# The last pair of token tiles in a seven-product block multiplication: its own order of products and PSUM tiles, and its stores halved between two queues

## The chip, the cores and the metric

The kernel runs on one core of a Trainium2 chip. The metric is the device time of one execution in microseconds (us); times of several runs are given as their median with the lowest and the highest. One further execution was recorded by the hardware profiler. All times inside it are counted from the start of its span, which runs from the first instruction to the last.

## The reference

An attention stage feeds a two-layer feed-forward stage. Batch 8, 12 heads, 448 tokens, head width 64; 3584 tokens of width 768 in all, inner width 2048.

```python
q_n, k_n = (rmsnorm(q, g_q), rmsnorm(k, g_k))
scores = scale * np.matmul(q_n, k_n.transpose(0, 1, 3, 2))
attn = softmax(scores)                      # max taken off, sums divided
x = np.matmul(attn, v)                      # then heads side by side: (B*S, H*D)
h = x @ w_in
g = np.maximum(h, 0.0) + alpha * np.minimum(h, 0.0)
out = (g @ w_out).astype(np.float32)
```

(`softmax` is written out in the reference.) The change touches only the last product, `g @ w_out`, for the last tokens.

## The kernel before

The order of all work is written out by hand: the kernel is traced under a manual schedule, and a planner ahead of the main loop spreads the feed-forward matmuls over the attention steps by estimated costs. Each engine runs its instructions in the program's order, and so does each queue of DMA issues. Loads and most stores are issued by SyncE (SP).

Feed-forward, first half (`up`, L475 to L498): for one block of 128 inner columns, TensorE (PE) makes `hT`, ScalarE (ACT) scales it by alpha, VectorE (DVE) takes the maximum, and the result is a row block of `gT`, held as 16 blocks of 128 inner columns by 896 tokens (two batches). Second half (`down`, L500): a tile of 128 tokens times a half of the output columns (384), 16 matmuls summed in one PSUM bank, copied to `osb` and stored.

For the last two batches, output tiles t = 1 to 6 are done another way, in pairs (1, 2), (3, 4) and (5, 6). Before them the remaining `up` blocks run, with what is left of tile 0, done the ordinary way, mixed in (L815 to L820, L1029). A pair of token tiles and the two halves of the inner columns make a 2 x 2 block matrix, the two halves of the inner columns and the two halves of the output columns another, and `quad` (L576) multiplies them by a Strassen-Winograd scheme: seven block products in place of eight. GpSimd (POOL) makes the sums of the weight blocks once (`mix_weights`, L537) and the sums s1 to s4 of the token blocks for each pair (`mix`, L559).

A block product (`product`, L600) is 8 matmuls of 128 x 128 by 128 x 384, issued at L602, into one PSUM bank. Two of the seven add onto a bank that holds an earlier product. Numbered as in the new code, with the order that `quad` has before (L614 to L641):

- m1: block (t, 0) times the first weight block, into bank x. ACT copies it to SBUF (L616).
- m6: s2 into bank y. DVE adds the copy and gives u2 (L619).
- m5: s1 into bank p, or, in the last pair, in two halves of 192 columns into two banks (`ps`).
- m7: s3 into bank z. DVE adds u2 and gives u3 (L624).
- m2: onto x. ACT copies it into an output tile (L627): output of tile t, left half. Two stores.
- then p + u3, with no product of its own (L631): output of tile t + 1, right half. Two stores.
- m4: onto z. DVE adds u2 (L635): output of tile t + 1, left half. Two stores.
- m3: s4 onto p. DVE adds u2 (L640): output of tile t, right half. Two stores; in the last pair it goes by halves of 192 columns, each with its own addition and two stores.

`send` (L568) stores a tile as two DMAs of 64 partitions each (L572): 96 KB each, 48 KB for a half of the columns. All are issued by SP, except that with `split` the second is issued by ACT; before the change only m3's halves in the last pair have that.

```python
(nc.scalar if split and half else nc.sync).dma_start(
    out=dst[:, c], in_=o[ds(64 * half, 64), c]
)
```

PSUM tiles come from three pools: `pss` (tag `sc`, two buffers of two banks), `psa` (tag `acc`, one buffer of two banks), `psf` (tag `mm`, two buffers of one bank). Pairs 1 and 5 take x, p from one `sc` tile and y, z from the other; pair 3 takes y, z from `acc` and x, p from `mm`. A reused buffer makes its first writer wait for the last reader of the tile before. The output tiles `osb` have four buffers; a buffer is free when its stores have landed.

The pairs run in the order 1, 3, 5 (L1033 to L1034), and nothing comes after pair 5.

Of the kernel before, what the change touches and what calls it, by code (L numbers as in the profile page):

```python
# [9 lines left out]
FP32 = mybir.dt.float32  # L10
# [11 lines left out]
def kernel(  # L22
# [12 lines left out]
    nc = tc.nc  # L35
# [9 lines left out]
    OH = DM // 2  # L45
# [14 lines left out]
    psa = ctx.enter_context(tc.tile_pool(name="psa", bufs=1, space=bass.MemoryType.PSUM))  # L60
# [495 lines left out]
    def block(t, f):  # L556
        return gT[:, ts(f, HF), ts(t, 128)]
# [10 lines left out]
    def send(b0, t, oh, o, c=slice(0, None), split=False):  # L568
        for half in range(2):
            bb, j = divmod(2 * t + half, J)  # L570
            dst = out4[b0 + bb, j, :, ts(oh, OH)]
            (nc.scalar if split and half else nc.sync).dma_start(  # L572
                out=dst[:, c], in_=o[ds(64 * half, 64), c]
            )

    def quad(b0, t, wide, last=False):  # L576

        s1, s2, s3, s4 = (mixes[t][:, n] for n in range(4))
        if wide:
            even, odd = (  # L580
                pss.tile([128, 2, 512], FP32, name="oq", tag="sc") for _ in range(2)
            )
            x, p = even[:, 0], even[:, 1]
        else:
            odd = psa.tile([128, 2, 512], FP32, name="oqa", tag="acc")
            x, p = (psf.tile([128, 512], FP32, name="oqm", tag="mm") for _ in range(2))
        y, z = odd[:, 0], odd[:, 1]
        full = (slice(0, OH),)
        ps = [p]
        if last:  # L590
            full = (slice(0, OH // 2), slice(OH // 2, OH))
            ps = [psf.tile([128, 512], FP32, name="oqm", tag="mm") for _ in range(2)]

        def whole(f, m):
            return lambda ft: w_out_sb[:, HF * f + ft, ts(m, OH)]

        def mixed(n):
            return lambda ft: tw[n, ft // QF][:, ft % QF]

        def product(bank, g, v, first, c=slice(0, OH)):  # L600
            for ft in range(HF):
                nc.tensor.matmul(  # L602
                    out=bank[:, c], lhsT=g[:, ft], rhs=v(ft)[:, c],
                    start=(first and ft == 0), stop=(ft == HF - 1),
                    skip_group_check=True,
                )

        def part(name):
            return ld.tile([128, OH], FP32, name=name, tag="qs", bufs=4)

        def result():
            return ffn.tile([128, OH], FP32, name="osb", tag="osb", bufs=4)

        product(x, block(t, 0), whole(0, 0), True)  # L614
        m1 = part("m1")
        nc.scalar.copy(out=m1, in_=x[:, :OH])  # L616
        product(y, s2, mixed(1), True)
        u2 = part("u2")
        nc.vector.tensor_add(out=u2, in0=y[:, :OH], in1=m1)  # L619
        for b, c in zip(ps, full):  # L620
            product(b, s1, mixed(0), True, c)
        product(z, s3, mixed(2), True)
        u3 = part("u3")
        nc.vector.tensor_add(out=u3, in0=z[:, :OH], in1=u2)  # L624
        product(x, block(t, 1), whole(1, 0), False)
        o = result()
        nc.scalar.copy(out=o, in_=x[:, :OH])  # L627
        send(b0, t, 0, o)
        o = result()
        for b, c in zip(ps, full):  # L630
            nc.vector.tensor_add(out=o[:, c], in0=b[:, c], in1=u3[:, c])  # L631
        send(b0, t + 1, 1, o)
        product(z, block(t + 1, 1), mixed(3), False)
        o = result()
        nc.vector.tensor_add(out=o, in0=z[:, :OH], in1=u2)  # L635
        send(b0, t + 1, 0, o)
        o = result()
        for b, c in zip(ps, full):
            product(b, s4, whole(1, 1), False, c)
            nc.vector.tensor_add(out=o[:, c], in0=b[:, c], in1=u2[:, c])  # L640
            send(b0, t, 1, o, c, last)  # L641

    def spin(count, wide=True):

# [11 lines left out]
    den_at, av_at, split = {}, {}, {}  # L656
# [5 lines left out]
    while m < NG * J or steps:  # L662
# [21 lines left out]
        while len(bursts[n]) < limit and m < NG * J:  # L684
            y, j = divmod(m, J)
# [91 lines left out]
    for b in range(B - 1):  # L777
# [9 lines left out]
        for n in range(lo, hi):  # L787
            clock += cost(n)
            free = True
            while ups or old or new:  # L790
                two = n in dens and pre(dens[n]) and len(gaps[n]) < 2
                if old and (not ups or (free or two) and (
                    wide(n) or len(old) > sum(wide(c) for c in range(n, hi))
                )):
                    u = old.pop(0)
                elif ups:
                    u = ups.pop(0)
                else:
                    u = new.pop(0)
# [31 lines left out]
    for n, g in enumerate((g_q, g_k)):  # L831
        for h in range(2):
            nc.gpsimd.dma_start(
                out=rows[NF + n : NF + n + 1, ds(64 * h, 64)], in_=g.unsqueeze(0)
# [9 lines left out]
    both, full, lo, hi = slice(0, 2), slice(0, J), slice(0, K0), slice(K0, J)  # L844
    for h in range(2):
        part_square("q", slice(h, h + 1), full, nc.scalar)
    for h in range(2):
# [13 lines left out]
        out=gain, in0=cols[:, NF : NF + 1], in1=cols[:, NF + 1 : NF + 2]  # L861
# [31 lines left out]
    for n in range(NB):  # L893
# [61 lines left out]
        if n in roots:  # L955
            y = roots[n]
# [41 lines left out]
        for k, (f, a) in enumerate(gaps[n]):  # L998
# [3 lines left out]
            else:  # L1002
                f(*a, spare)
                done += 1
                if n in jobs and not (lead and done < 5) and (
                    n < av_at[2 * G - 1] or done % 2
                ):
                    g, c = jobs[n].pop(0)
# [3 lines left out]
                while late and done == late[0][0]:  # L1012
                    _, g, c = late.pop(0)
# [19 lines left out]
    for t in (1, 3, 5):  # L1033
        quad(B - 2, t, t != 3, t == 5)  # L1034
# [30 lines left out]
```

## Time and profile before

| what | value |
|---|---|
| median of 3 runs | 426.19 us (425.29 to 426.56) |
| the profiled execution, device time | 425.32 us |
| its span | 423.6 us (423.55 in the trace) |
| busy PE, ACT, DVE, POOL | 97%, 66%, 53%, 68% of the span |
| granted PE clock, mean | 0.996 |
| PE op at L602 in the chain that ended last | tiles `oq` 4%, `oqm` 2% of the span |
| stores at the end (L572) | 24 issued by SP, 2 by ACT |
| a store of 96 KB by SP, issue to landing | 2.2 us median |

How to read it: the device time is somewhat longer than the span. In the timeline, a line gives start, length, engine, source line, operation, and the tiles written and read; `x8` are eight instructions in a row, and the length is then from the first's start to the last's end. The name SPq or ACTq stands for an instruction that the engine's queue runs itself, here the issue of a DMA; such instructions are not counted as busy, so an engine can be idle in the page while its queue is what others wait for. What a DMA moves goes on after its issue, and a store has landed when its semaphore has come.

### The profile page before, as it was taken

Reading aid. Unit: us, or ns where it says so; the run is one execution under the profiler, and the core shown is the slowest. Engines: PE = TensorE matmul, PEld = TensorE weight load, DVE = VectorE, ACT = ScalarE, POOL = GpSimd, SP = SyncE. Lnnn points to the kernel's source line nnn. Section 1 sums busy time; section 2 is a strip of 40 time slices with the busy share of each in tenths; the row PEclk is TensorE's granted clock in tenths of the full one; section 3 lists DMA queues with packets and bytes.
Section 4 is the critical chain, followed back from the end, with each engine's and each line's share of the span. In section 5 each row is a group of like instructions: output and inputs, shape, how many; then the busy total and the mean of one; then the engine's idle time right before and its main releaser. Section 6 shows DMA issues by size and latency. Waiting matters only on the chain.

```text
span 423.6 us, 11137 instructions
## 1 busy us (share of the span) xinstructions
PE 410.0 (97%) x4731; PEld 214.3 (51%) x4731; DVE 224.4 (53%) x335; ACT 278.4 (66%) x390; POOL 290.1 (68%) x201
## 2 busy tenths in 40 slices
PE   8789999999999999999999999999999999999994
PEld 3344454544455454544555445554555545555663
DVE  3875964556464636636565454557463353355232
ACT  5898887778856686668846677667856577255100
POOL 6689994494996289382993569572982999940960
PEclk9999999999999999999999999999999999999998
DMA  8999999999638975568456974547225501100233
GB/s 192 239 244 226 211 192 201 232 163 243 121 82 124 197 126 127 86 135 182 80 117 111 174 177 107 101 85 150 46 44 100 118 2 22 39 19 2 56 85 85
DMA packets 68530, 53.37 MB, mean 126 GB/s; under 512 B 35568, under 2 KB 68480, under 8 KB 68480
## 3 DMA queue, kind: packets, MB, share of 16 engines
q1 hardware_dynamic: 53760, 39.83, 43.0%
q0 software_dynamic: 13984, 11.81, 18.7%
q10 hardware_dynamic: 736, 1.02, 1.0%
q8 instruction: 37, 0.61, 0.6%
q14 instruction: 13, 0.11, 0.1%
HBM read 45.62 MB, written 11.01 MB: 134 GB/s over the span
## 4 chain that ended last, share of the span: by engine, by line
PE 83%; ACT 6%; POOL 4%; DVE 4%; issue 1%; ACTq 1%; POOLq 0%
PE op L508 23%; PE hT L454 21%; PE hTa L454 8%; PE sc L329 8%; PE av L368 5%; PE opa L508 4%; PE oq L602 4%; PE dn L368 3%; ACT expT L343 3%; POOL rden L356 2%; PE avb L368 2%; PE oqm L602 2%; ACT ah L494 2%; PE dnb L389 2%; DVE gT L498 1%
## 5 line engine op out<-in xcount | busy, mean ns | idle before, releaser
L343 ACT ACTIVATE expT<-sc,expb 128x896 f16<-128x896 f32 x168 | 161.3, 1003 | 42.5 <-PE sc L329 42.2
L179 POOL TENSOR_TENSOR qs<-nat,rr 128x896 f16<-128x896 f32 x41 | 68.4, 1690 | 81.8 <-issue 39.3
L454 PE MATMUL hT<-xT,w_in_sb 128*128 128x448 f16 x558 | 115.7, 353 | 0.8 <-DVE gT L498 0.5
L454 PEld LDWEIGHTS <-w_in_sb 128*128 128x128 f16 x768 | 73.2, 98 | 74.0 <-issue 9.4
L508 PE MATMUL op<-w_out_sb,gT 128*128 128x384 f16 x592 | 101.4, 326 | 0.5 <-DVE gT L498 0.5
L508 PEld LDWEIGHTS <-gT 128*128 128x128 f16 x704 | 66.1, 98 | 53.0 <-issue 11.8
L494 ACT ACTIVATE ah<-hT,cols 128x448 f16<-128x448 f32 x92 | 58.1, 632 | 41.8 <-PE hT L454 40.9
L498 DVE TENSOR_TENSOR gT<-hT,ah 128x448 f16<-128x448 f32 x93 | 57.8, 623 | 49.2 <-ACT ah L494 48.4
L155 POOL TENSOR_TENSOR sq<-nat 128x896 f32<-128x896 f32 (+1 forms) x47 | 75.4, 1625 | 8.2 <-DMA nat<-in_q_dram 8.0
L356 POOL TENSOR_TENSOR rden<-rden,expT 128x896 f32<-128x896 f32 x30 | 56.8, 1894 | 2.4
L329 PE MATMUL sc<-qT,kT 64*32 64x448 f16 (+1 forms) x1092 | 53.9, 356 | 4.4 <-ACT expT L343 2.2
L163 DVE TENSOR_REDUCE ss<-sq 128x14 f32<-128x896 f32 (+1 forms) x48 | 48.9, 1038 | 1.5 <-POOL sq L155 1.3
L520 DVE COPY osb<-op 128x384 f32<-128x384 f32 x37 | 20.5, 555 | 54.4 <-PE op L508 54.0
L454 PE MATMUL hTa<-xT,w_in_sb 128*128 128x448 f16 x198 | 42.8, 352 | 0.0
L329 PEld LDWEIGHTS <-kT 64*32 64x32 f16 (+1 forms) x1092 | 16.9, 93 | 35.6 <-issue 29.0
L494 ACT ACTIVATE ah<-hTa,cols 128x448 f16<-128x448 f32 x33 | 20.9, 634 | 15.3 <-PE hTa L454 15.2
L498 DVE TENSOR_TENSOR gT<-hTa,ah 128x448 f16<-128x448 f32 x33 | 20.6, 623 | 17.6 <-ACT ah L494 17.0
L439 DVE TENSOR_TENSOR xT<-av,rden 128x896 f16<-128x896 f32 x16 | 17.5, 1091 | 21.4 <-ACT rden L410 15.4
L368 PEld LDWEIGHTS <-vt 64*32 64x32 f16 (+1 forms) x1260 | 21.4, 94 | 12.7 <-issue 2.5
L368 PE MATMUL av<-expT,vt 64*32 64x448 f16 (+1 forms) x812 | 26.2, 349 | 0.0
L508 PE MATMUL opa<-w_out_sb,gT 128*128 128x384 f16 x112 | 19.4, 327 | 0.0
L563 POOL TENSOR_TENSOR gs<-gT 128x1024 f16<-128x1024 f16 x3 | 6.4, 2117 | 16.6 <-DVE gT L498 16.6
(98 smaller groups left out, 330.5 us busy)
## 6 DMA issues: line engine op xcount, KB each, us to landing
out_dram<-osb SPq DMA_DIRECT2D x110, 96.0 KB, 2.2
nat<-in_q_dram SPq DMA_DIRECT2D x46, 224.0 KB, 4.3
nat<-in_k_dram SPq DMA_DIRECT2D x46, 224.0 KB, 4.6
vt<-in_v_dram POOLq DMA_DIRECT2D x16, 336.0 KB, 6.1
w_in_sb<-in_moe_w_in_dram POOLq DMA_DIRECT2D x12, 256.0 KB, 7.4
w_out_sb<-in_moe_w_out_dram POOLq DMA_DIRECT2D x4, 768.0 KB, 11.3
nat<-in_q_dram ACTq DMA_DIRECT2D x2, 224.0 KB, 4.9
nat<-in_k_dram ACTq DMA_DIRECT2D x2, 224.0 KB, 6.4
```

Of the source, the lines that this page charges most:

```text
L155: nc.gpsimd.tensor_mul(out=sqf[:, c], in0=src[:, c], in1=src[:, c])
L163: nc.vector.tensor_reduce(out=o[:, c], in_=sqs[y, nm][:, c], axis=AXIS_X, op=ALU.add)
L179: eng.tensor_mul(out=t.rearrange("p j h d -> p h j d"), in0=nat[y, nm], in1=rr_t[y][:, "qk".index(nm)].unsqueeze(3).broadcast_to((128, 2, ...
L329: nc.tensor.matmul(out=sc[ds(64 * g + m * c, m), par, :S].rearrange("p (j c) -> p j c", j=J), lhsT=kT[ds(64 * par, 64), j, g, ts(c, m)], r ...
L343: nc.scalar.activation(out=expT[y][:, j], in_=scs[y, j][:, :, :S], func=AF.Exp, scale=QK_SCALE, bias=expb[:, 0:1],)
L356: nc.gpsimd.tensor_add(out=s, in0=e[:, 0] if j == 1 else s, in1=e[:, j])
L368: nc.tensor.matmul(out=accs[g][ds(m * h, m), :S], lhsT=weights(g, y, par, ts(c, m), j), rhs=expT[y][ds(64 * g, 64), j, par, :], start=(j = ...
L454: nc.tensor.matmul(out=hT[:, :S], lhsT=w_in_sb[:, g * G + i, ts(ft, 128)], rhs=xT[b][:, g, i, :], start=(i == 0 and g == 0), stop=(i == G ...
L494: nc.scalar.activation(out=ah, in_=hT[:, :S], func=AF.Copy, scale=alpha_sb[:, ft : ft + 1])
L498: nc.vector.tensor_max(out=gT[:, ft, ds((b & 1) * S, S)], in0=hT[:, :S], in1=ah)
L508: nc.tensor.matmul(out=ops[c][:, :PW], lhsT=gT[:, ft, ts(t, 128)], rhs=w_out_sb[:, ft, ds(oh * OH + c * PW, PW)], start=(ft == 0), stop=(f ...
L602: nc.tensor.matmul(out=bank[:, c], lhsT=g[:, ft], rhs=v(ft)[:, c], start=(first and ft == 0), stop=(ft == HF - 1), skip_group_check=True,)
```

## The change

For pairs 1 and 3 the new code issues the same as before; the body of `quad` is cut into small functions that are called in a list. For the last pair (t = 5):

- The order of products is m1, m6, m2, m7, m5, then the output without a product of its own ("fourth"), m4, m3. Before, it was m1, m6, m5, m7, m2, fourth, m4, m3.
- Bank y comes from `psa` (tag `acc`) in place of the second `sc` tile, in which z stays. x stays in the first `sc` tile, and the two banks of `ps` in `mm`.
- Every output tile is sent with `split`: the first 64 partitions by SP, the others by ACT. Before, that held for m3's halves alone. SP issues 3 stores of 96 KB and 2 of 48 KB for this pair, ACT as many.

The number of matmuls, copies, additions and stores, and their sizes, are the same.

```diff
     def quad(b0, t, wide, last=False):
 
         s1, s2, s3, s4 = (mixes[t][:, n] for n in range(4))
-        if wide:
+        full = (slice(0, OH),)
+        if wide or last:
...
-        full = (slice(0, OH),)
         ps = [p]
         if last:
+            y = psa.tile([128, 2, 512], FP32, name="oqa", tag="acc")[:, 0]
             full = (slice(0, OH // 2), slice(OH // 2, OH))
...
+        def m5():
+            for b, c in zip(ps, full):
+                product(b, s1, mixed(0), True, c)
+
+        def m7():
+            product(z, s3, mixed(2), True)
+            u[3] = part("u3")
+            nc.vector.tensor_add(out=u[3], in0=z[:, :OH], in1=u[2])
+
+        def m2():
+            product(x, block(t, 1), whole(1, 0), False)
+            o = result()
+            nc.scalar.copy(out=o, in_=x[:, :OH])
+            send(b0, t, 0, o, split=last)
+
+        def fourth():
+            o = result()
+            for b, c in zip(ps, full):
+                nc.vector.tensor_add(out=o[:, c], in0=b[:, c], in1=u[3][:, c])
+            send(b0, t + 1, 1, o, split=last)
+
+        def m4():
+            product(z, block(t + 1, 1), mixed(3), False)
+            o = result()
+            nc.vector.tensor_add(out=o, in0=z[:, :OH], in1=u[2])
+            send(b0, t + 1, 0, o, split=last)
...
+        for f in (
+            (m1, m6, m2, m7, m5, fourth, m4, m3) if last
+            else (m1, m6, m5, m7, m2, fourth, m4, m3)
+        ):
+            f()
```

The functions m1, m6 and m3, left out here, hold the lines that were there before.

More of the change, by code (lines that the diff above doesn't have):

```diff
@@ L612, in result @@
             return ffn.tile([128, OH], FP32, name="osb", tag="osb", bufs=4)
[L614 to L641, printed above, removed]
+        u = {}
+        def m1():
+            product(x, block(t, 0), whole(0, 0), True)
+            u[1] = part("m1")
+            nc.scalar.copy(out=u[1], in_=x[:, :OH])
+        def m6():
+            product(y, s2, mixed(1), True)
+            u[2] = part("u2")
+            nc.vector.tensor_add(out=u[2], in0=y[:, :OH], in1=u[1])
@@ new lines, in m4, with m3 @@
+        def m4():
[3 more added lines that the diff above has]
+            send(b0, t + 1, 0, o, split=last)
+        def m3():
+            o = result()
+            for b, c in zip(ps, full):
+                product(b, s4, whole(1, 1), False, c)
+                nc.vector.tensor_add(out=o[:, c], in0=b[:, c], in1=u[2][:, c])
+                send(b0, t, 1, o, c, last)
+        for f in (
[3 more added lines that the diff above has]
+            f()
```

## The prediction

> **What bounds the kernel now.** I read the chain of waits first, then the store issues in the last 10 us, then the end of the span. Over the span PE is busy 97%, and the chain of waits over the last 13 us says the same of the last pair: products follow each other without a gap until 417.80, then one VectorE addition ends at 418.19.
>
> ```profile
> 410.93 0.33 PE oq L602 x2
> 411.25 1.32 PE oqm L602 x16
> 412.57 3.90 PE oq L602 x24
> 416.47 1.33 PE oqm L602 x16
> 417.80 0.02 issue
> 417.83 0.36 DVE osb L640
> ```
>
> The columns are start, length and what. A product of 384 columns costs 1.30 us, one in two halves 1.32. The span, though, ends at 423.55: 5.36 us lie behind the last addition, and no compute engine works in them. The timeline of SP's queue, of ACT, and of VectorE over the last pair tells what does:
>
> ```profile
> 415.75 5.22 SPq L572 DMA_DIRECT2D out_dram<-osb  x8
> ```
> ```profile
> 415.25 0.48 ACT L627 COPY osb<-oq 128x384 f32<-128x384 f32 x1 [4.79 <-PE oq L602]
> 417.56 1.19 ACTq L572 DMA_DIRECT2D out_dram<-osb  x2
> ```
> ```profile
> 413.91 0.56 DVE L624 TENSOR_TENSOR u<-oq,u 128x384 f32<-128x384 f32 x1 [1.99 <-PE oq L602]
> 414.50 0.62 DVE L631 TENSOR_TENSOR osb<-oqm,u 128x192 f32<-128x192 f32 x2
> 416.51 0.56 DVE L635 TENSOR_TENSOR osb<-oq,u 128x384 f32<-128x384 f32 x1 [1.39 <-PE oq L602]
> 417.17 0.36 DVE L640 TENSOR_TENSOR osb<-oqm,u 128x192 f32<-128x192 f32 x1
> 417.83 0.36 DVE L640 TENSOR_TENSOR osb<-oqm,u 128x192 f32<-128x192 f32 x1 [0.30 <-PE oqm L602]
> ```
>
> SP issues eight stores back to back from 415.75 to 420.97. The L631 result is complete at 415.12, but its stores stand behind those of the ACT copy, which is complete only at 415.73 (SP stood idle for it from 412.67). From there SP is always late: the last data are ready at 418.19, and the last store is issued at 420.42, 2.23 us later. The single issues near the end:
>
> ```profile
> 417.56 0.55 ACTq L572 DMA_DIRECT2D out_dram<-osb  x1
> ...
> 417.87 0.47 SPq L572 DMA_DIRECT2D out_dram<-osb  x1
> ...
> 419.77 0.55 SPq L572 DMA_DIRECT2D out_dram<-osb  x1
> ...
> 420.42 0.56 SPq L572 DMA_DIRECT2D out_dram<-osb  x1
> ```
>
> One step of SP is 420.42 - 419.77 = 0.65 us (0.60 to 0.68 in the pair before); I take 0.64. The last store lands 1.97 us after its issue, at 422.39, and from there to the end of the span are 1.16 us of waits and barriers. So the bound of the tail is **the number of issues on SP's queue after 415.75**; ACT's queue takes two.
>
> **The change, part by part.** Order of the products: m1, m6, m2, m7, m5, m4, m3 in place of m1, m6, m5, m7, m2, m4, m3. All are the same 72 matmuls (five products of 8, two of 16), so PE still runs from 408.65 to 417.80 if nothing makes it wait: product ends 409.95, 411.25, 412.55 (m2), 413.85 (m7), 414.51 and 415.17 (m5's halves), 416.47, 417.80. Its waits, each against this timetable:
> - m6 writes a new bank of the tile that pair 3 used; that is free when pair 3's L635 addition ends (407.39 + 0.56 = 407.95), and m6 starts at 409.95: 2.0 us to spare.
> - m2 adds onto x after ACT has copied it (409.99 to 410.47), and starts at 411.25: 0.78 to spare. Here m2 was moved forward by two products, so this is the thinnest new margin; behind it on PE stands all the rest.
> - m7 no longer shares a tile with m6, so it no longer waits for the addition into u2 (over at 411.92).
> - m5's second bank is free after pair 3's L640 (408.69 + 0.56 = 409.25), needed at 414.5.
> - m4 needs z, read by the u3 addition: 413.89 + 0.56 = 414.45 against 415.17, 0.7 to spare, as before. m3's halves need the two L631 additions, 414.9 and 415.6 against 416.47 and 417.13.
>
> So order and tiles cost PE nothing, and the last addition still ends at 418.19. If a margin failed, each us of PE's stall would be a us of the end.
>
> The copy of m2 moves from 415.25 to 412.55 + 0.08 = 412.63, and ends at 413.11. ACT has nothing else to do then. Its stores go out at 413.13; SP is free, as pair 3's eight stores end at 412.67 (they run from 406.63 for 6.03 us). The two L631 additions now wait for m5's halves and end at 415.21 + 0.36 = 415.57 instead of 415.12; 0.45 later, but their stores are issued at 415.6, no longer at 416.97 and 417.87.
>
> Stores: three that SP issued go to ACT. SP has five (m2 413.13, fourth 415.60, m4, m3, m3), ACT the other five. m4's data are ready at 417.07, as before: issue 417.10 on both. The next step is 417.74 (m3's first half, ready 417.53), the last 418.38 (ready 418.19). Behind the waiting stores on ACT stand only stores, then its closing drain (0.40 us), so nobody but the end waits for them. Each queue also waits for an older store that uses the same semaphore; the youngest of these is m2's, landed by about 415.4.
>
> Landing: 1.97 us on SP with nothing beside it, 2.15 for the second of ACT's two beside SP. As two go out together now I take 2.15: 418.38 + 2.15 = 420.53, plus the unchanged 1.16 is 421.69. **Sum: 423.55 - 421.69 = 1.86 us less.**
>
> Bounds of what the trace does not show, two queues issuing in step. From below: issue as soon as the data are ready, 418.22, and landing 1.97: end 421.35, 2.20 less. From above: SP has a gap of 0.36 us ahead of its 417.87 issue, just after ACT's 417.56, where 0.10 is usual; if each of two steps loses this 0.26, and landing takes the 2.40 of ACT's first store, the end is 418.90 + 2.40 + 1.16 = 422.46, 1.09 less. Nearest to my value is the ordinary step: the start of the kernel has SP and ACT issue loads at the same 3.70, in 0.60 and 0.63 us.
>
> Taken apart, the halved stores alone (old order) would give SP 415.75, 416.39, 417.10, 417.74, 418.38: the same last issue. The order alone gives SP two stores each at 415.60, 417.10 and on to 419.02: 1.40 less. The parts overlap; what the order adds beside the split is only that transfers start earlier.
>
> The transfers themselves are the cover that could go. The windows table has for the stretch of the stores:
>
> ```profile
> 416.85:421.40 4.55, 0.94 (x12) 0.71 (x9) 0.93 (x3) 0.00 (x0) 0.00 (x0) 0.90 0.74 164
> ```
>
> The last two columns are the DMA engines' busy share and GB/s: 0.74 x 4.55 = 3.37 us of all engines for 746 KB, so 0.44 us for a 98 KB store against SP's 0.64 a step. One queue leaves a quarter idle, and the split fills it.
>
> A rule of the Trainium skill speaks against the split: "DMA: Bandwidth & Descriptors", section "Issuing engines are not separate DMA queues", says that DMAs of all engines share the same 16 engines, and that issuing from several saves only the sequencer's time, usually small beside the transfer. The trace agrees on what is saved but not that it is small here (0.64 against 0.44). By the rule the split would be worth nothing and the order's 1.40 would stay, 424.8.
>
> **Own time and median.** The profiled execution took 425.32 us, 1.77 more than its span; 425.32 - 1.86 = 423.5. It is one of the short ones: the three runs shown have a median of 426.19 (425.29 to 426.56). Taking the gain off the median: 426.19 - 1.86 = **424.3**.
>
> **Rivals.**
> 1. *The sum holds*: 424.3, between 2.20 and 1.4 less. For it: ready data and free queues at each step. 70 in 100.
> 2. *The engines or the two queues hold each other up*: m4's and m3's stores, 393 KB, start together at about 418.2 (issue 417.10 and 1.1 us more: the windows table has no traffic from 415.75 to 416.85); at 164 GB/s they need 2.4, so 420.6; landing comes 0.4 behind the last packets (422.0 and 422.39 before), so the end is 422.2: 1.4 less. With the delays of the upper bound 1.09. And one issue can stall: pair 3's last store took 1.65 where 0.59 is usual, while a block of instructions was loaded; 1.06 of that in the last steps leaves 1.86 - 1.06 = 0.8, so 425.4. 20 in 100, the middle at 425.1.
> 3. *It does not do what it says*: SP is no longer the bound but the end stays, because something fixed lies behind the last product. Against: SP's last issue and the end are a plain landing and 1.16 apart. 426.2. 6 in 100.
> 4. *Slower*: ACT's queue becomes the new slow one. Its last three stores cannot start before 417.10; ACT ends later than SP did when its last issue passes 423.55 - 1.16 - 2.15 = 420.24, so from (420.24 - 417.10) / 2 = 1.57 us an issue. If ACT took the 1.65 of the slowest issue each time, its five would start at 413.13, 415.60, 417.25, 418.90 and 420.55; end 420.55 + 2.15 + 1.16 = 423.86, 0.3 slower, 426.5 (and 428.1 at 2.2 us an issue). Against: 0.53 and 0.55 in its two stores, 0.63 to 0.86 in its loads. 4 in 100.
>
> **How the numbers follow.** About 0.3% (1.28 us) is what a measurement can tell from nothing. Rival 1 lies beyond it nearly always, and so does the 1.4 of rival 2: faster 0.77, same 0.19, slower 0.04. The range: best case 426.19 - 2.20 = 424.0, less the 0.9 by which a median can come out as low as the lowest run, 423.1; upper end the stalled issue of rival 2 with a little of the runs' spread, 425.7.
>
> **What would show it.** Right: PE's last product still ends within 0.1 of 417.80 after the same start; ACT's copy near 412.6; five stores on each queue, last issues at 418.2 to 418.5; end 3.2 to 3.6 us behind them. Wrong: a gap in PE ahead of m2 or m6 (order), issues of 0.8 us or more on either queue or gaps of 0.3 between them (rivals 2 and 4), landings over 2.4 us (transfers), or an unchanged end with early issues (rival 3).

## The result, and the profile after

| | before | after |
|---|---|---|
| median, 11 runs each | 426.19 us (425.24 to 426.75) | 423.71 us (423.47 to 425.34) |
| ratio | | 0.9953 (0.9941 to 0.9966) |
| the profiled execution: device time, span | 425.32, 423.55 us | 425.34, 423.52 us |
| end of the last VectorE addition | 418.19 | 419.96 |
| **tail**: from there to the end of the span | 5.37 us | 3.56 us |

The two profiled executions are equal in length but not alike: the one after reaches the last pair 1.78 us later. The windows tables, after first, then before (the third column from the right is the mean granted clock of TensorE in the stretch):

```profile
10.00:20.00 10.00, 8.65 (x62) 3.51 (x61) 8.15 (x14) 7.81 (x11) 5.78 (x8) 0.83 1.15 243
20.00:30.00 10.00, 8.61 (x115) 3.30 (x114) 6.91 (x9) 9.15 (x13) 7.96 (x11) 0.83 1.18 236
...
11.30:14.70 3.40, 3.40 (x18) 1.15 (x10) 1.81 (x4) 1.91 (x2) 2.95 (x4) 0.50 1.09 236
...
21.50:24.90 3.40, 3.40 (x12) 0.62 (x12) 2.15 (x3) 2.72 (x5) 1.36 (x4) 0.51 1.09 233
```
```profile
10.00:20.00 10.00, 7.67 (x66) 3.44 (x64) 9.29 (x17) 8.92 (x13) 6.74 (x9) 1.00 1.15 238
20.00:30.00 10.00, 8.87 (x191) 4.46 (x198) 7.20 (x9) 9.73 (x15) 7.94 (x11) 1.00 1.14 249
```

In the execution after, the mean of 0.83 comes from two stretches of 3.4 us at half clock; the execution before has none, and a second profiled execution of the changed kernel (`both`, below) has one and reaches the last pair 0.81 us later than before. The runs of either kernel fall into groups some 0.9 us apart, which fits such stretches, though only the profiled executions show them. Nothing of the change is there. What it did to the end is read with the last addition as the zero of time: 5.37 - 3.56 = 1.81 us. The lowest runs differ by about the same, 425.24 - 423.47 = 1.77; the medians, which move with all that lies ahead of the last pair, by 2.48.

The chain of waits of the kernel after, over the last pair:

```profile
410.43 1.30 PE oq L603 x8
411.73 1.30 PE oqa L603 x8
413.03 2.60 PE oq L603 x16
415.63 1.32 PE oqm L603 x16
416.95 1.30 PE oq L603 x8
418.25 1.33 PE oqm L603 x16
419.58 0.02 issue
419.60 0.36 DVE osb L658
```

The order is m1, m6 (bank in `oqa`), m2 and m7, m5, m4, m3, without a gap: 419.58 - 410.43 = 9.15 us, as before (417.80 - 408.65). The timelines of ACT and of SP's queue:

```profile
414.41 0.48 ACT L639 COPY osb<-oq 128x384 f32<-128x384 f32 x1 [2.17 <-PE oq L603]
414.92 6.00 ACTq L572 DMA_DIRECT2D out_dram<-osb  x5
```
```profile
414.91 5.72 SPq L572 DMA_DIRECT2D out_dram<-osb  x5
```

Five issues on each queue, and now with room between them: they are spread over 5.7 and 6.0 us, where eight of SP's stood back to back in 5.22. The two additions of the fourth output, which now wait for m5's halves, on VectorE:

```profile
416.32 0.36 DVE L645 TENSOR_TENSOR osb<-oqm,u 128x192 f32<-128x192 f32 x1
416.98 0.36 DVE L645 TENSOR_TENSOR osb<-oqm,u 128x192 f32<-128x192 f32 x1 [0.30 <-PE oqm L603]
```

The second ends at 417.34, and its stores go out at once (417.37 on both queues). The last two issues of each queue, single lines of the timeline:

```profile
419.44 0.54 SPq L572 DMA_DIRECT2D out_dram<-osb  x1
...
419.47 0.80 ACTq L572 DMA_DIRECT2D out_dram<-osb  x1
...
420.08 0.55 SPq L572 DMA_DIRECT2D out_dram<-osb  x1
...
420.36 0.55 ACTq L572 DMA_DIRECT2D out_dram<-osb  x1
```

SP's last issue comes 0.12 us after the last addition (2.23 before), ACT's 0.40 after it, because ACT's issue before took 0.80 us. ACT's last store, in the list of DMA issues (the last number is us from issue to landing), is the last to land:

```profile
out_dram<-osb ACTq DMA_DIRECT2D x1, 48.0 KB, 1.9
```

More closely it takes 1.94 and lands at 422.30, and 1.22 us of waits and barriers follow.

### The profile page after: what moved, and what is told of

Same layout as the page of the kernel before. It is cut to its first block, busy times and chain, and to the rows that moved or that the text cites. A ratio compares the mean times of both kernels' runs of the same rounds, so it can differ in the third digit from the quotient of the medians.

```text
span 423.5 us, 11140 instructions
## 1 busy us (share of the span) xinstructions
PE 411.3 (97%) x4731; PEld 214.7 (51%) x4731; DVE 224.7 (53%) x335; ACT 278.4 (66%) x390; POOL 290.9 (69%) x201
## 4 chain that ended last, share of the span: by engine, by line
PE 85%; ACT 6%; DVE 4%; POOL 2%; DMA 1%; issue 1%; POOLq 0%; ACTq 0%
PE op L508 23%; PE hT L454 21%; PE sc L329 8%; PE hTa L454 8%; PE av L368 5%; PE opa L508 4%; ACT expT L343 3%; PE oq L603 3%; PE dn L368 3%; POOL rden L356 2%; PE avb L368 2%; PE oqm L603 2%; ACT ah L494 2%; PE dnb L389 2%; PE spin L671 1%; DVE gT L498 1%
## 5 line engine op out<-in xcount | busy, mean ns | idle before, releaser
L329 PE MATMUL sc<-qT,kT 64*32 64x448 f16 (+1 forms) x1092 | 54.9, 359 | 3.5 <-ACT expT L343 1.4
```

What stands on the lines that cost most here:

```text
L329: nc.tensor.matmul(out=sc[ds(64 * g + m * c, m), par, :S].rearrange("p (j c) -> p j c", j=J), lhsT=kT[ds(64 * par, 64), j, g, ts(c, m)], r ...
```

## The experiments

Each experiment is told by the change against the kernel after ("the whole change") and by its tail, which came out alike to 0.01 us in two profiled executions of the whole change. "Last issue" is counted from the end of the last addition. The lowest time is that of 4 to 7 timed runs (10 in `pool_m4`, 11 before and after), the ratio that to the runs of the kernel before made beside it (their lowest: 425.21 to 425.24).

| kernel | last issue SP, ACT | tail | lowest us | ratio |
|---|---|---|---|---|
| before | +2.23, +0.03 | 5.37 | 425.24 | |
| whole change | +0.12, +0.40 | 3.56 | 423.47 | 0.9953 (0.9941 to 0.9966) |
| both (the same again) | +0.12, +0.40 | 3.57 | 423.65 | 0.9972 (0.9961 to 0.9983) |
| split_alone | +0.32, +0.61 | 3.78 | 423.63 | 0.9964 (0.9950 to 0.9977) |
| order_alone | +0.95, +0.03 | 4.09 | 423.98 | 0.9969 (0.9952 to 0.9986) |
| all_on_sp | +3.43, none | 6.59 | 426.43 | 1.0040 (1.0027 to 1.0052) |
| old_tile | +0.12, +0.40 | 3.56 | 423.63 | 0.9963 (0.9949 to 0.9977) |
| m2_on_sp | +0.12, +0.40 | 3.58 | 423.45 | 0.9959 (0.9946 to 0.9973) |
| one_issue | -0.63, +0.03 | 14.83 | 434.74 | 1.0226 (1.0209 to 1.0242) |
| pool_m4 | +0.03, +0.03 | 5.06 | 424.93 | 0.9987 (0.9977 to 0.9998) |
| m3_one_store | +0.03, +0.03 | 3.78 | 423.72 | 0.9965 (0.9953 to 0.9977) |
| pool_m2 | +0.37, +0.40 | 3.96 | 423.92 | 0.9973 (0.9961 to 0.9985) |

**both.** No edit.

> The changed kernel once more, so that the parts run beside it on one chip. Measure: the tail, from the end of the last VectorE addition to the end of the span (5.36 us before, 3.54 in its profile: 423.5 - 419.96). All theories: tail 3.4 to 3.7, the last product 9.15 us after the first of the last pair starts, time 1.6 to 2.1 us below before in runs with the same granted clock.

Every issue of the last pair is within 0.01 us of the first execution's place, the tail 3.57. The times spread more: 423.65 to 424.53 in seven runs, with a ratio of 0.9972. A ratio of a few runs is coarser here than a tail.

**split_alone.**

```diff
-            (m1, m6, m2, m7, m5, fourth, m4, m3) if last
+            (m1, m6, m5, m7, m2, fourth, m4, m3) if last
...
-            y = psa.tile([128, 2, 512], FP32, name="oqa", tag="acc")[:, 0]
```

> Old order and old tiles, every store of the last pair halved between SP and ACT. Theory (the number of issues on SP's queue sets the end): stores of m2 go out when ACT's copy is done, 2.46 us before the last addition ends, and the queues are level again by m4; last issues within 0.1 of those of the whole change, tail 3.5 to 3.6. Transfer rival (all eight stores' data now start in the last 2.4 us): 786 KB at 0.44 us per 98 KB is 3.5 us from the first packets, so the tail is 3.8 to 3.9. Order rival (the earlier copy is what gains): tail 5.0 or more.

Tail 3.78: the split alone brings 1.59 of the 1.81 us, so the order rival falls. But 3.78 is the number I gave to the transfers, and the queues show another cause. The timelines of SP and of ACT:

```profile
415.66 3.29 SPq L572 DMA_DIRECT2D out_dram<-osb  x5
```
```profile
415.66 3.59 ACTq L572 DMA_DIRECT2D out_dram<-osb  x5
```

Five issues in a row on both: they start together when m2's copy is done, and are not level by m4. Single issues, first two of SP, then two of ACT:

```profile
416.24 0.54 SPq L572 DMA_DIRECT2D out_dram<-osb  x1
...
417.19 0.47 SPq L572 DMA_DIRECT2D out_dram<-osb  x1
```
```profile
416.30 0.75 ACTq L572 DMA_DIRECT2D out_dram<-osb  x1
...
417.80 0.80 ACTq L572 DMA_DIRECT2D out_dram<-osb  x1
```

ACT's second issue took 0.75 and its fourth 0.80 us; SP stood 0.42 between its second and third, 0.2 of it after m4's data were there (416.97). The last issues are 0.20 (SP) and 0.21 (ACT) later than in the whole change, and the last store lands 1.94 to 1.95 after its issue in both. So the 0.22 are issues, not transfers.

**order_alone.**

```diff
-            send(b0, t, 0, o, split=last)
+            send(b0, t, 0, o)
```

(the same for the fourth output and m4).

> New order and new tile, stores as before (SP issues all but the second store of m3's halves). Theory: SP has four issues from the moment m4 is ready, 0.64 us apart, so the last one 0.83 us after the last addition ends; 1.97 landing and 1.16 to the end: tail 3.96, 0.4 above the whole change and 1.4 below before. Order rival: tail 3.5 as the whole change. Split rival (order worth nothing): 5.36.

Tail 4.09, against 3.96 expected: 1.28 less than before. SP's last issue is at +0.95 in place of +0.83, as its issue before that took 0.75. The order rival (3.5) and the split rival (5.36) both fall: each part alone takes most of the queue's backlog away, and they overlap.

**all_on_sp.**

```diff
-                send(b0, t, 1, o, c, last)
+                send(b0, t, 1, o, c)
```

with old order and tile and without the other splits: the kernel before with ACT's two stores on SP.

> The kernel before, but with the two stores that ACT issues there given to SP as well: ten issues on SP in place of eight. Theory: two more steps of 0.64 to 0.65 us behind 420.42, tail 5.36 + 1.29 = 6.65. Rival (the landings or the transfers set the end, not the issues): tail as before, 5.2 to 5.5, as the same bytes go out.

The timeline of SP's queue and VectorE's last addition:

```profile
415.91 6.44 SPq L572 DMA_DIRECT2D out_dram<-osb  x10
```
```profile
417.98 0.36 DVE L657 TENSOR_TENSOR osb<-oqm,u 128x192 f32<-128x192 f32 x1 [0.30 <-PE oqm L602]
```

Ten issues in 6.44 us, where eight took 5.22: two more cost 1.22, and the tail grew by as much, 5.37 to 6.59 (1.29 expected). With the same bytes and the same data times the end follows the number of issues on the queue. Nor do transfers pile up behind the queue: each of the ten stores landed 1.93 to 2.24 after its own issue. This is the plainest evidence of the bound.

**old_tile.** The line with `y = psa.tile(...)` left out, all else as in the whole change.

> The whole change, but bank y stays beside z in the old tile, so m7 waits for the addition into u2. Theory: that addition is over 0.6 us before m7 starts, so no gap in PE, the last product ends 9.15 us after the pair starts, tail 3.56, time as the whole change. Rival (the tile is what keeps PE running in the new order): a gap of PE ahead of m7 and a time later by it, 0.3 us or more.

Tail 3.56 and no gap in PE. The new tile is worth nothing here.

**m2_on_sp.**

```diff
-            send(b0, t, 0, o, split=last)
+            send(b0, t, 0, o)
```

(m2 alone).

> The whole change, but both stores of m2 go out on SP, so that ACT has four stores. In the whole change ACT's fourth store (m3's first half) takes 0.79 us to issue where 0.50 to 0.55 is usual, and ACT's last issue is 0.28 behind SP's. Place theory (the long issue belongs to the fourth store in ACT's program): the long one is now the last, ACT's last issue comes at +0.12 from the last addition, tail 3.3 to 3.5. Contention theory (the long one comes where both queues issue m3's first half at once while a block of instructions is loaded): m3's first half is long again, tail 3.56 as in the whole change. For SP both give one issue more long before the end, which costs nothing.

ACT has four stores, and the long issue (0.79) is again that of m3's first half, now its third: the place theory falls. Contention gave the right number, but its second half, the block of instructions loaded at the same time, does not hold in all kernels: ACT's 0.75 in split_alone, SP's 0.75 in order_alone and one of ACT's in pool_m2 (0.78) overlap no such load. What makes an issue take 0.75 to 0.80 in place of 0.50 to 0.55 stays open.

**one_issue.** `send` given one DMA for both halves in the last pair:

```diff
+        if eng is not None:
+            bb, j = divmod(2 * t, J)
+            dst = out4[b0 + bb, ds(j, 2), :, ts(oh, OH)]
+            eng.dma_start(out=dst[:, :, c], in_=o[:, c])
+            return
```

> The whole change, but each tile of the last pair goes out as one store of 128 partitions (2 x 64 rows in memory) in place of two of 64: m2, m4 and m3's second half on ACT, the others on SP. Five issues in place of ten. Theory that the number of issues is all that counts: each queue is free when its data come, last issue at +0.03, landing 2.1 to 2.3 for twice the bytes, tail 3.2 to 3.5. Rival, by the Trainium skill (DMA: Bandwidth & Descriptors, on how many engines a DMA uses: the largest number up to 16 that divides the slowest dimension on both sides): only 2 of the 16 engines carry each store, 8 times slower; m4's 196 KB then take some 7 us from -0.1, tail 7 or more.

The queues were free in time, last issues -0.63 and +0.03, and the tail was 14.83. Two stretches of the windows table of this kernel:

```profile
422.00:426.00 4.00, 0.00 (x0) 0.00 (x0) 0.00 (x0) 0.00 (x0) 0.00 (x0) 0.50 0.13 48
426.00:430.00 4.00, 0.00 (x0) 0.00 (x0) 0.00 (x0) 0.00 (x0) 0.00 (x0) 0.50 0.13 47
```

The share of the 16 engines is 0.13, that is 2 of 16, at 47 to 48 GB/s, and it stays there while several stores are under way. The rule cited in the expectation (the Trainium skill, "DMA: Bandwidth & Descriptors", section "Why a DMA increments its semaphore by 16 and not by 1") is borne out. My 7 us were too few, as I counted m4's store alone: all five together get no more than two engines, and 786 KB at 48 GB/s are 16 us from the first at about 414. Fewer issues are no gain where the shape of the DMA loses engines.

**pool_m4.**

```diff
-            send(b0, t + 1, 0, o, split=last)
+            send(b0, t + 1, 0, o, pool=last)
```

where `pool` picks `nc.gpsimd` for both halves.

> The whole change, but m4's two stores are issued by POOL, idle since its last sum, so that SP and ACT have nothing behind which m3's halves queue. Theory: SP's and ACT's last issues at +0.03, landing 2.0, their part of the tail 3.2. POOL issues m4 at -1.09 and 0.7 us later; its loads elsewhere take 0.7 us an issue. If POOL's stores land within 2.5 us of their issue they are not last and the tail is 3.2 to 3.4; if they take 3 or more, the tail is set by them, 3.8 or more.

SP and ACT are on time (+0.03 both), but the tail is 5.06. POOL's closing instructions, as the source view of that line lists them (ns shortest/median/longest, then first and last start):

```profile
L1084 POOLq DRAIN  x3: 46/103/4348, 418.3 to 423.1; - x3
```

The drain of 4.35 us from 418.28 ends at 422.63, 3.8 after the end of POOL's last issue, and the end waits for it: SP is done with its own closing waits at 421.89, and POOL's next step, which follows such a moment by 0.02 in the whole change, comes 0.78 after it. That is a cost that I had not on the list, some 0.75 us. The other half of the loss is landing, and not POOL's alone. POOL's second store, issued at -0.06, lands 2.68 later, and m3's second halves on SP and ACT land 2.76 and 2.92 after their issue, where the whole change has 1.97 and 1.94; the last landing is 2.95 after the last addition in place of 2.34. Six stores were issued here within 0.85 us, in the whole change the same six within 1.49; whether that or POOL's queue delays them is not shown. Without the drain the tail would be some 4.3 (an estimate, 5.06 less 0.75): in the range expected for late landings.

**m3_one_store.**

```diff
-                send(b0, t, 1, o, c, last)
+                if not last:
+                    send(b0, t, 1, o, c)
+            if last:
+                send(b0, t, 1, o, split=True)
```

> The whole change, but m3's tile is stored once whole, by a pair of 96 KB stores after its second half, in place of two pairs of 48 KB. Eight issues in place of ten. If the number of issues behind m4 is what still costs: last issues at +0.03 on both queues in place of +0.12 and +0.40, tail 3.3 to 3.4. If the landing of a pair issued at the same instant costs it back (m4's pair in the whole change lands 2.15 and 2.49 after its issue, m3's second half 1.97 and 1.94): 0.03 + 2.49 + 1.22, tail 3.7, 0.15 above the whole change.

Tail 3.78, the second of the two. Both last issues are 0.03 after the last addition, yet ACT's 96 KB land 2.38 after their issue (in the whole change 48 KB in 1.94), and the waits after the landing take 0.13 longer. With the queues level, storing m3 by halves is worth 0.2 us.

**pool_m2.** As pool_m4, with m2's stores in place of m4's.

> The whole change, but POOL issues m2's two stores in place of SP and ACT; pool_m4 had it issue m4's, and its tail was 5.06, not from a late landing but from POOL's closing drain, which lasted until 3.8 us after POOL's last issue (in the kernel before it lasts 3.1 us beyond POOL's last sum, hidden behind the stores). If that drain is the cause, it now ends near -0.5 from the last addition and the tail is as in the whole change, 3.5 to 3.6. If a store from POOL as such costs the end (its slower landing, or its share of the engines), the tail stays above 4.

Tail 3.96: between the two. The drain ends at -0.21 and no longer sets the end, as expected; but SP stands 0.42 us ahead of m3's first half, and two of ACT's issues take 0.78, so the last issues are at +0.37 and +0.40, and the last landing at 2.61. That POOL's drain was a part of what pool_m4 lost is consistent with this. So is that its landings were late because POOL's stores came last: here m3's second halves land 2.03 and 2.21 after their issue. It is not more than that.

None of these beats the whole change by what can be measured.

## Why the prediction was right, point by point

- *What bounds the kernel* was right: the issues on SP's queue after m2's copy. all_on_sp added two and paid 1.22 us for them, with no store landing later after its issue.
- *Order and tiles cost PE nothing*: right. 9.15 us before and after, none of the margins failed, and the tile could have stayed (old_tile).
- *The timetable* was right. Taking 1.78 off the times after: copy 412.63 (412.63 predicted), m2's stores 413.13 (413.13), fourth 415.59 (415.60), m4 417.09 (417.10), SP's last 418.30 (418.38).
- *The last issue* was mis-sized on ACT: 418.58 against 418.38, for the issue of 0.80. *Landing* was mis-sized the other way: 1.94 against 2.15, and the rest 1.22 against 1.16. Together 3.56 against 418.38 + 2.15 + 1.16 - 418.19 = 3.50, so 1.81 us less where 1.86 were forecast. That the sum came within 0.05 us is partly luck: an issue 0.20 too late and a landing 0.21 too short cancel. The term that was too small is the plain 0.64 per issue; with both queues in use, single issues took 0.75 to 0.80.
- *The signs of being wrong* were not all absent. ACT's issue of 0.80 and two of its landings, 2.46 and 2.49 for the fourth output and m4, reach the marks that the prediction set for rival 2, and ACT's last issue lies just outside the 418.2 to 418.5 given. So something of rival 2's kind did occur, with its cause open; it cost 0.20 us at the end, not the 0.5 to 1.1 that rival 2 priced. The late landings were of earlier stores and cost nothing.
- *The halved stores alone give the same last issue*: wrong by 0.2 us. I let every step take 0.64 from 415.75, and the queues are level only with next to no delay in any of four steps. What the order adds is slack: in the whole change each queue is idle for 1.0 us before m4 (SP 1.03, ACT 0.98), in which delays of the size seen vanish.
- *SP's gap of 0.36 as the price of two queues*: wrong. The gap is SP's own. In order_alone it stands at the same place of SP's program, ahead of its fourth store of the pair, while ACT issued nothing:

```profile
415.49 1.30 SPq L572 DMA_DIRECT2D out_dram<-osb  x2
```

  The two issues take 0.47 each, so 0.36 lie between. In all_on_sp, where ACT issues no store of this pair, the gap there is 0.37. What it is stays open.
- *The transfers* were the cover: it held here and in split_alone, where the last landing is no later after its issue than in the whole change. In pool_m4 the last landings were late by 0.8 to 1.0 us, so the room is not wide.
- *The rule of the Trainium skill* ("DMA: Bandwidth & Descriptors", section "Issuing engines are not separate DMA queues") that several issuing engines save only issue time agrees with what the split saved; that this is usually small did not hold. split_alone shows 1.59 us for it: at the end of a kernel with small stores, the issue time saved was what bounded.
- *The median*: 423.71 against 424.3, inside the range. Most of the 0.6 between them lies ahead of the last pair: the lowest runs differ by 1.77 and the tails by 1.81, near the 1.86 forecast.

## What to carry to other kernels

Behind the last compute instruction, count the stores still to be issued on each queue and multiply by the step, here 0.65 us on average for a store of 96 or 48 KB (5.85 us from the first to the last of ten on SP in all_on_sp); that backlog, not the bytes, was what could be taken off the tail. Take it away by a second queue, and give the queues idle time ahead of the last data, as an order that finishes outputs earlier does, since single issues can be late by 0.25 to 0.4. Fewer and larger DMAs did not help in either form tried: merged into one, a store got 2 of the 16 engines (one_issue), and with m3 stored once the larger store landed later (m3_one_store).

## What the runs showed of the hardware that was not expected

- POOL's closing drain lasts 3.1 us beyond its last sum in the kernel before, 3.8 beyond the end of its last DMA issue in pool_m4 and 3.3 in pool_m2. It set the end in pool_m4 alone, where POOL's last issue ended 2.5 us before the last landing; in pool_m2 it ended 6.1 us before.
- Pair 3's last store took 1.65 us to issue before, 1.59 in split_alone and 1.53 in all_on_sp, each time while a block of 16 KB of instructions was being loaded (from -7.3 of the last addition). In the other kernels that load came at the end of the issue or after it (from -6.65 on, the issue starting at -7.17), and the issue took 0.59 to 0.61.
